# Float64 weights to float32 on the chip: another sequence of operations per piece

## The chip, the cores and the metric

The kernel runs on one core of one Trainium2 chip. The metric is the device time of one execution in microseconds (us), of which less is better. A core has a matrix engine (TensorE, PE in the profile, with its weight loads as PEld), a vector engine (VectorE, DVE), a scalar engine (ScalarE, ACT), a general engine (GpSimd, POOL) and a queue that here only issues DMAs (SyncE, SP). Each engine works through its own instructions in order; they wait for one another by semaphores.

## The reference

Attention with queries pooled in pairs, then two feed-forward blocks:

```python
q_pool = q.reshape(B, H, S // 2, 2, D).mean(axis=3)
attn = softmax(q_pool @ k.T / sqrt(D))            # 16 heads, 576 queries, 1152 keys, D = 64
x = (attn @ v) as [1152 tokens, 512]
h = x @ w_in                                      # MoE 1: 512 -> 2048 -> 512
x = where(h > 0, h, exp(min(h, 0)) - 1) @ w_out
xn = x / sqrt(mean(x * x) + 1e-6) * rms_g         # MoE 2: 512 -> 1536 -> 512
y = (silu(xn @ w_gate) * (xn @ w_val)) @ w_out2
```

The activations are float32. The five weight matrices arrive as float64 and are brought to float32 on the chip.

## The kernel before

Every float32 matrix is split into two float32r parts (a rounded one and the rest), and each product is three matmuls (lines 168 to 170). A weight is worked on in 68 pieces of [128, 512] words: 16 of `w_in`, 16 of `w_out`, 12 each of the gate, value and output weights of MoE 2. `Stream` (line 72) turns a piece into parts operation by operation. For one piece it records, with a `yield` after each: one ACT operation on the upper words (`Square`, line 111), a DVE shift (line 113), then the last three steps of the piece before (permission to take the buffers of its parts, an ACT copy to the rounded part `wh` at line 142, a POOL subtraction to the rest `wl` at line 62), and then five more DVE operations (lines 118, 121, 124, 126, 130). That makes 10 steps, six of them DVE operations on 128x512. The raw words are in `wr` (two buffers, loaded by SP, line 89), the results in `wt` (two buffers), helpers in `we` (two) and `wx` (one).

What the rest of the program does decides where these steps fall: `ws.step(i, k)` (line 149) records up to k of them between other work, and nothing if the next step would take a buffer of parts that is not allowed yet. With piece i in use, the stream may go as far as piece i + 8 (`WB`).

- Attention (lines 475 to 501): 72 tiles, 9 to a pair of heads. A tile has 6 score matmuls (L280), a scaled copy with its minimum on DVE (L284), the exponential on ACT (L289), 9 transposes (L298), copies on ACT (L306) and subtractions on DVE (L68), and 8 matmuls with v (L324). POOL splits q, k and v for the pair to come. In the last 33 tiles one step of the stream falls to each.
- MoE 1 hidden, first half and second half (line 593): 8 blocks by 3 chunks of 384 tokens each; 12 matmuls a chunk, then `elu` (line 181): two ACT operations, one DVE operation (L188), an ACT copy and a subtraction on POOL (in the second half on DVE for one chunk in three). Four steps of the stream per chunk.
- MoE 1 out, first half and second half (line 603): 24 products of 12 matmuls in each half, four steps of the stream per product, fewer at the end of the second half, where sums of squares (`Norm`, L562 to L569) are formed between the products.
- MoE 2 (line 646): pairs of products with `swiglu`, then the output products. Seven steps per pair.

A product's results go to one of 8 PSUM banks. PE may run ahead of the others by those banks; the out products need all hidden blocks.

## Time and profile before

| | |
|---|---|
| three timed runs | 724.67, 725.07, 725.17 us, median 725.07 |
| span of the profiled execution | 722.7 us |
| PE busy | 689.2 us (95%), 4243 matmuls |
| DVE busy | 614.9 us (85%), 965 instructions |
| ACT busy | 415.6 us (58%), 855 instructions |
| POOL busy | 390.7 us (54%), 326 instructions |

The span runs from the first to the last instruction of one more execution, taken with the profiler; about 2.4 us of a timed run lie outside of it. A busy engine is one whose instruction has started and not ended, waiting inside the instruction included. Matmuls overlap, so their count in a stretch says more than their busy time. The profile's stages, by the lines that run in them: attention 0 to 256 us, MoE 1 hidden first half 256 to 322, its out products to 368, hidden second half to 437, out products and norm to 506, MoE 2 to the end.

### The profile page before, as it was taken

Reading aid. Unit: us, or ns where it says so; the run is one execution under the profiler, and the core shown is the slowest. Engines: PE = TensorE matmul, PEld = TensorE weight load, DVE = VectorE, ACT = ScalarE, POOL = GpSimd, SP = SyncE. Lnnn points to the kernel's source line nnn. Section 1 sums busy time; section 2 is a strip of 40 time slices with the busy share of each in tenths; the row PEclk is TensorE's granted clock in tenths of the full one; section 3 lists DMA queues with packets and bytes.
Section 4 is the critical chain, followed back from the end, with each engine's and each line's share of the span. In section 5 each row is a group of like instructions: output and inputs, shape, how many; then the busy total and the mean of one; then the engine's idle time right before and its main releaser. Section 6 shows DMA issues by size and latency. Waiting matters only on the chain.

```text
span 722.7 us, 11547 instructions
## 1 busy us (share of the span) xinstructions
PE 689.2 (95%) x4243; PEld 673.3 (93%) x4243; DVE 614.9 (85%) x965; ACT 415.6 (58%) x855; POOL 390.7 (54%) x326
## 2 busy tenths in 40 slices
PE   7999999999999999969999968979999999999997
PEld 6999999989899999859999968979999999999997
DVE  7988989898999869999999999955999999999700
ACT  5888988889798865663356663424444443432300
POOL 4988889788896226754335453523445544443300
PEclk9999999999999999989999998989999999999999
DMA  5333322533331001223322212200222222222300
GB/s 196 116 96 135 98 84 83 172 131 107 105 98 48 1 30 60 87 70 105 117 92 85 87 59 88 88 30 1 87 88 89 88 88 88 88 88 88 124 34 33
DMA packets 21607, 62.34 MB, mean 86 GB/s; under 512 B 2736, under 2 KB 4784, under 8 KB 21552
## 3 DMA queue, kind: packets, MB, share of 16 engines
q1 hardware_dynamic: 21552, 61.62, 25.9%
q8 instruction: 33, 0.54, 0.3%
q14 instruction: 22, 0.18, 0.1%
HBM read 59.25 MB, written 2.36 MB: 85 GB/s over the span
## 4 chain that ended last, share of the span: by engine, by line
PE 74%; DVE 19%; ACT 3%; issue 3%; DMA 1%; SPq 0%; POOL 0%; DVEq 0%; ACTq 0%; POOLq 0%
PE b L169 15%; PE b L168 15%; PE b L170 15%; PE s L280 10%; PE o L324 9%; PE t L298 8%; DVE wt L121 3%; DVE wt L118 3%; DVE p L284 2%; DVE ptl L68 2%; DVE e L188 2%; DVE wx L124 2%; DVE wx L126 1%; DVE wt L130 1%; DVE wt L113 1%
## 5 line engine op out<-in xcount | busy, mean ns | idle before, releaser
L62 POOL TENSOR_TENSOR wl<-wt,wh 128x512 fp32r<-128x512 f32 x68 | 106.1, 1561 | 111.6 <-ACT wh L142 60.2
L168 PE MATMUL b<-xh,wh 128*128 128x384 f32 x468 | 157.7, 337 | 2.1 <-DVE e L188 1.5
L170 PE MATMUL b<-xh,wl 128*128 128x384 f32 x468 | 157.3, 336 | 0.0
L169 PE MATMUL b<-xl,wh 128*128 128x384 f32 x468 | 157.1, 336 | 0.0
L284 DVE TENSOR_SCALAR_CACHE_REDUCE p<-s 128x1152 f32<-128x1152 f32 x72 | 97.2, 1352 | 17.5 <-PE s L280 17.4
L68 DVE TENSOR_TENSOR ptl<-t,pth 128x384 fp32r<-128x384 f32 x216 | 106.5, 547 | 2.7 <-ACT pth L306 2.0
L280 PE MATMUL s<-kd,qt 128*128 128x384 f32 x480 | 98.6, 343 | 5.4 <-DVE p L284 4.8
L306 ACT CAST pth<-t 128x384 fp32r<-128x384 f32 x216 | 89.2, 488 | 24.1 <-PE t L298 23.5
L121 DVE SCALAR_TENSOR_TENSOR wt<-we,wt 128x512 f32<-128x512 f32 x68 | 95.5, 1404 | 4.5 <-ACT sqm L562 0.5
L289 ACT ACTIVATE p<-p,st 128x1152 f32<-128x1152 f32 x72 | 91.4, 1269 | 5.8 <-DVE p L284 5.5
L168 PEld LDWEIGHTS b<-xh,wh 128*128 128x128 f32 x468 | 88.0, 188 | 3.5 <-DVE e L188 2.5
L280 PEld LDWEIGHTS s<-kd,qt 128*128 128x128 f32 x480 | 81.5, 188 | 9.3 <-DVE p L284 6.5
L170 PEld LDWEIGHTS b<-xh,wl 128*128 128x128 f32 x468 | 88.0, 188 | 0.3 <-POOL wl L62 0.3
L169 PEld LDWEIGHTS b<-xl,wh 128*128 128x128 f32 x468 | 88.0, 188 | 0.0
L298 PE MATMUL t<-ident,p 128*128 128x128 f32 x648 | 85.3, 275 | 0.1
L324 PE MATMUL o<-pth,vd 128*128 128x256 f32 (+1 forms) x288 | 84.4, 315 | 0.0
L298 PEld LDWEIGHTS t<-ident,p 128*128 128x128 f32 x648 | 74.0, 141 | 6.3 <-DVE ptl L68 3.9
L324 PE MATMUL o<-ptl,vd 128*128 128x256 f32 (+1 forms) x288 | 78.5, 295 | 0.0
L168 PE MATMUL b<-gh,wh 128*128 128x384 f32 x180 | 64.3, 357 | 14.1 <-ACT gh L189 10.8
L142 ACT CAST wh<-wt 128x512 fp32r<-128x512 f32 x68 | 42.1, 619 | 59.5 <-DVE wt L130 58.4
L111 ACT ACTIVATE we<-wr 128x512 f32<-128x512 f32 x68 | 45.8, 674 | 47.2 <-DMA wr<-in_w_dram 16.1
L62 POOL TENSOR_TENSOR gl<-e,gh 128x384 fp32r<-128x384 f32 x37 | 46.8, 1265 | 41.4 <-ACT gh L189 39.7
(114 smaller groups left out, 1414.5 us busy)
## 6 DMA issues: line engine op xcount, KB each, us to landing
wr<-in_w_dram SPq DMA_DIRECT2D x32, 512.0 KB, 3.2
rawk<-in_k_dram SPq DMA_DIRECT2D x32, 288.0 KB, 2.9
rawq<-in_q_dram SPq DMA_DIRECT2D x15, 576.0 KB, 3.9
wr<-in_wg_dram SPq DMA_DIRECT2D x12, 512.0 KB, 3.2
wr<-in_wv_dram SPq DMA_DIRECT2D x12, 512.0 KB, 3.2
wr<-in_wo_dram SPq DMA_DIRECT2D x12, 512.0 KB, 3.3
rawv<-in_v_dram SPq DMA_DIRECT2D x16, 288.0 KB, 2.8
out_dram<-o SPq DMA_DIRECT2D x12, 192.0 KB, 1.9
```

Of the source, the lines that this page charges most:

```text
L62: G.tensor_tensor(out=o, in0=i, in1=f(h), op=ALU.subtract)
L68: V.tensor_tensor(out=o, in0=i, in1=f(h), op=ALU.subtract)
L121: V.scalar_tensor_tensor(out=f(t), in0=e, scalar=TINY64 * TINY64, in1=f(t), op0=ALU.is_ge, op1=ALU.mult)
L168: PE.matmul(out, lhsT=wh[:, k, :], rhs=ah, start=first and k == 0, stop=False)
L169: PE.matmul(out, lhsT=wh[:, k, :], rhs=al, start=False, stop=False)
L170: PE.matmul(out, lhsT=wl[:, k, :], rhs=ah, start=False, stop=last and k == 3)
L280: PE.matmul(s[:, m, 0:384], lhsT=a, rhs=b[:, 384 * m:384 * m + 384], start=n == 0, stop=n == len(parts) - 1)
L284: V.tensor_scalar(out=pt, in0=s[:, :, 0:384], scalar1=-0.0625, scalar2=None, op0=ALU.mult, op1=ALU.min, accum_out=st[p][:, 0, TILES[i][4], :])
L289: T.activation(out=pt, in_=pt, func=AF.Exp, scale=-1.0, bias=st[p][:, 0, TILES[i][4], :], accum_out=st[p][:, 1, TILES[i][4], :])
L298: PE.transpose(ps[:, k, :], src[:, 128 * b:128 * b + 128], ident)
L306: T.copy(oh, re(ps))
L324: PE.matmul(self.o[:, 0:self.N], lhsT=v[:, b, :], rhs=(pth, ptl)[u][:, g["buf"], b, g["c0"]:320], start=self.n == 0, stop=self.n == 17)
```

## The change

A piece is brought to float32 by another sequence. On ACT, `Abs` of an eighth of the upper words goes straight to `wt`. On DVE: the lower words, scaled and added to a constant, to `we`; `wt` limited from both sides; `wt` shifted left by three bits; the sign merged in from the upper words; and an integer add of `wt` and `we`. That is five DVE operations instead of six: three with one tensor input, one with two, and the add. `wx` is gone. The steps of a piece are 9 instead of 10. The rest of the kernel stands as it was (its comments are gone, which shifts lines by one or two).

```diff
-                    e = wp.tile([128, 512], F32, tag="we", name="we", bufs=2)
+                    e = wp.tile([128, 512], U32, tag="we", name="we", bufs=2)
                     t = wp.tile([128, 512], U32, tag="wt", name="wt", bufs=2)
-                    x = wp.tile([128, 512], U32, tag="wx", name="wx", bufs=1)
-                    T.activation(out=e, in_=f(hi), func=AF.Square)
+                    T.activation(out=f(t), in_=f(hi), func=AF.Abs, scale=0.125)
                     yield
-                    V.tensor_scalar(out=t, in0=hi, scalar1=3, scalar2=0x3FFFFFF8,
-                                    op0=ALU.logical_shift_left, op1=ALU.bitwise_and)
+                    V.tensor_scalar(out=f(e), in0=lo, scalar1=2.0 ** -27, scalar2=2.0 ** 25,
+                                    op0=ALU.mult, op1=ALU.add)
                     yield
                     if tail:
                         yield from tail
-                    V.scalar_tensor_tensor(out=t, in0=hi, scalar=0xC0000000, in1=t,
-                                           op0=ALU.bitwise_and, op1=ALU.bitwise_or)
+                    V.tensor_scalar(out=f(t), in0=f(t), scalar1=LEAST64, scalar2=MOST64, op0=ALU.max, op1=ALU.min)
                     yield
-                    V.scalar_tensor_tensor(out=f(t), in0=e, scalar=TINY64 * TINY64, in1=f(t),
-                                           op0=ALU.is_ge, op1=ALU.mult)
+                    V.tensor_scalar(out=t, in0=t, scalar1=3, scalar2=None, op0=ALU.logical_shift_left)
                     yield
-                    V.tensor_scalar(out=x, in0=t, scalar1=0xFF800000, scalar2=None, op0=ALU.bitwise_and)
-                    yield
-                    V.scalar_tensor_tensor(out=f(x), in0=lo, scalar=2.0 ** -52, in1=f(x), op0=ALU.mult, op1=ALU.mult)
+                    V.scalar_tensor_tensor(out=t, in0=hi, scalar=0x80000000, in1=t,
+                                           op0=ALU.bitwise_and, op1=ALU.bitwise_xor)
                     self.load(i + 3)
                     yield
+                    V.tensor_tensor(out=t, in0=t, in1=e, op=ALU.add)
                     w = f(t)
-                    V.tensor_tensor(out=w, in0=w, in1=f(x), op=ALU.add)
```

Since `ws.step` counts steps, the instructions also move. In attention two of the stream's loads come ahead of a load of v on SP's queue that they stood behind. Three other places show what moves. `e` is elu's tile, `b` a PSUM bank, `wt`, `we`, `wx` and `wr` the stream's.

DVE in MoE 1's first hidden half, from its first chunk; before:

```order
L188 SCALAR_TENSOR_TENSOR e_3553<-e_3553,b_3540 128x384
L118 SCALAR_TENSOR_TENSOR wt_3510<-wr_3053,wt_3510 128x512
L121 SCALAR_TENSOR_TENSOR wt_3510<-we_3509,wt_3510 128x512
L124 TENSOR_SCALAR wx_3511<-wt_3510 128x512
L126 SCALAR_TENSOR_TENSOR wx_3511<-wr_3053,wx_3511 128x512
L188 SCALAR_TENSOR_TENSOR e_3578<-e_3578,b_3565 128x384
L130 TENSOR_TENSOR wt_3510<-wt_3510,wx_3511 128x512
L113 TENSOR_SCALAR wt_3590<-wr_3501 128x512
L188 SCALAR_TENSOR_TENSOR e_3606<-e_3606,b_3593 128x384
```

and now:

```order
L187 SCALAR_TENSOR_TENSOR e_3544<-e_3544,b_3531 128x384
L120 TENSOR_SCALAR wt_3496<-wt_3496 128x512
L122 TENSOR_SCALAR wt_3496<-wt_3496 128x512
L124 SCALAR_TENSOR_TENSOR wt_3496<-wr_2921,wt_3496 128x512
L128 ISA wt_3496<-wt_3496,we_3495 128x1024
L187 SCALAR_TENSOR_TENSOR e_3569<-e_3569,b_3556 128x384
L115 TENSOR_SCALAR we_3579<-wr_3310 128x512
L187 SCALAR_TENSOR_TENSOR e_3596<-e_3596,b_3583 128x384
```

A piece's conversion ends one elu earlier, and the integer add stands there as an instruction of its own kind over 1024 elements a partition, the half-words of 512 words. From the first elu to the last of this half there are 51 operations of the stream on DVE before and 45 now.

DVE in MoE 1's second hidden half, three chunks in its middle; before:

```order
L113 TENSOR_SCALAR wt_4791<-wr_4714 128x512
L188 SCALAR_TENSOR_TENSOR e_4809<-e_4809,b_4796 128x384
L118 SCALAR_TENSOR_TENSOR wt_4791<-wr_4714,wt_4791 128x512
L121 SCALAR_TENSOR_TENSOR wt_4791<-we_4790,wt_4791 128x512
L68 TENSOR_TENSOR gl_3539<-e_4809,gh_3538 128x384
L124 TENSOR_SCALAR wx_4792<-wt_4791 128x512
L126 SCALAR_TENSOR_TENSOR wx_4792<-wr_4714,wx_4792 128x512
L188 SCALAR_TENSOR_TENSOR e_4834<-e_4834,b_4821 128x384
L130 TENSOR_TENSOR wt_4791<-wt_4791,wx_4792 128x512
L113 TENSOR_SCALAR wt_4846<-wr_4769 128x512
L188 SCALAR_TENSOR_TENSOR e_4862<-e_4862,b_4849 128x384
```

and now:

```order
L115 TENSOR_SCALAR we_4715<-wr_4640 128x512
L69 TENSOR_TENSOR gl_3530<-e_4705,gh_3529 128x384
L187 SCALAR_TENSOR_TENSOR e_4732<-e_4732,b_4719 128x384
L187 SCALAR_TENSOR_TENSOR e_4751<-e_4751,b_4738 128x384
L120 TENSOR_SCALAR wt_4716<-wt_4716 128x512
L122 TENSOR_SCALAR wt_4716<-wt_4716 128x512
L124 SCALAR_TENSOR_TENSOR wt_4716<-wr_4640,wt_4716 128x512
L128 ISA wt_4716<-wt_4716,we_4715 128x1024
L187 SCALAR_TENSOR_TENSOR e_4776<-e_4776,b_4763 128x384
```

With 9 steps to a piece the stream has come to the end of its buffers by here: after five operations in two chunks comes a chunk with none. In the whole half there are 56 operations of the stream before and 40 now.

ACT in the first hidden half, at the start of a piece, with the engines and queues that an instruction waits for; before:

```order
L189 CAST gh_3538<-e_3553 128x384 [waits DVE_49]
L111 ACTIVATE we_3589<-wr_3501 128x512 [waits DMAHW0_49]
L184 ACTIVATE e_3606<-b_3593 128x384 [waits PE_49,Pool_49]
L185 ACTIVATE e_3606<-e_3606 128x384 [waits Activation_49]
L189 CAST gh_3538<-e_3578 128x384 [waits DVE_49]
```

and now:

```order
L188 CAST gh_3529<-e_3544 128x384 [waits DVE_49]
L113 ACTIVATE wt_3580<-wr_3310 128x512 [waits DMAHW0_49,Pool_49]
L183 ACTIVATE e_3596<-b_3583 128x384 [waits PE_49]
L184 ACTIVATE e_3596<-e_3596 128x384 [waits Activation_49]
L188 CAST gh_3529<-e_3569 128x384 [waits DVE_49]
```

The ACT operation on the upper words stands at the same place, but it writes `wt` now and waits for POOL's subtraction on the piece two before, which reads the same buffer.

## Rows read from the trace of the kernel before

**Rows 1.** Windows: stretch, length, busy us (instructions) per engine, TensorE clock, DMA share, GB/s.

```profile
262.00:322.00 60.00, 52.80 (x298) 51.20 (x296) 56.31 (x71) 40.72 (x85) 39.12 (x30) 0.99 0.22 71
300.00:330.00 30.00, 22.41 (x107) 20.74 (x106) 29.52 (x37) 16.85 (x35) 19.85 (x15) 0.89 0.22 71
330.00:360.00 30.00, 30.00 (x174) 30.00 (x173) 28.48 (x40) 11.65 (x22) 8.75 (x7) 1.00 0.33 109
368.00:437.00 69.00, 59.81 (x333) 57.74 (x332) 65.27 (x92) 45.41 (x94) 34.63 (x26) 0.98 0.26 85
410.00:440.00 30.00, 20.81 (x101) 18.81 (x100) 28.15 (x41) 17.87 (x38) 14.99 (x12) 0.90 0.21 71
460.00:480.00 20.00, 15.39 (x79) 14.98 (x78) 13.76 (x20) 6.45 (x13) 8.09 (x7) 0.83 0.16 54
506.00:690.00 184.00, 184.00 (x1060) 184.00 (x1059) 169.53 (x232) 70.25 (x137) 80.46 (x55) 1.00 0.27 90
```

**Rows 2.** Waits of PE: who for whom, us in total, times, longest.

```profile
PE b L168 <- ACT gh L189: 10.8, 2, 5.6
PE b L569 <- DVE sq L564: 5.4, 2, 4.6
PE b L168 <- DVE e L188: 4.8, 5, 1.7
```

**Rows 3.** Chain of work that ended last, shares by line, 396 to 437 us.

```profile
by line: issue 19.4%; DVE wt L118 17.3%; DVE wt L121 16.7%; DVE e L188 13.7%; DVE wx L124 8.1%; DVE wt L130 6.9%; DVE wx L126 5.4%; DVE gl L68 5.2%; DVE wt L113 3.5%; PE b L169 1.7%; ACT wh L142 1.5%; ACT gh L189 1.3%; POOL gl L62 1.2%; DVE
```

**Rows 4.** The clock while PE starts again: windows of 1 us.

```profile
321.00:322.00 1.00, 0.28 (x1) 0.28 (x1) 0.97 (x3) 0.84 (x2) 0.77 (x2) 0.63 0.00 0
327.00:328.00 1.00, 1.00 (x5) 1.00 (x4) 1.00 (x1) 0.22 (x1) 1.00 (x2) 0.50 0.07 16
```

**Rows 5.** Durations by line: ns min/median/max, first and last start us, shape.

```profile
L113 DVE TENSOR_SCALAR wt<-wr x68: 409/419/1266, 141.4 to 677.8; 128x512 uint32<-128x512 uint32 x68
L118 DVE SCALAR_TENSOR_TENSOR wt<-wr,wt x68: 671/693/1545, 144.5 to 678.3; 128x512 uint32<-128x512 uint32 x68
L121 DVE SCALAR_TENSOR_TENSOR wt<-we,wt x68: 678/1591/1675, 148.4 to 679.1; 128x512 f32<-128x512 f32 x68
L124 DVE TENSOR_SCALAR wx<-wt x68: 411/428/1405, 151.8 to 680.7; 128x512 uint32<-128x512 uint32 x68
L126 DVE SCALAR_TENSOR_TENSOR wx<-wr,wx x68: 629/693/1649, 155.5 to 681.1; 128x512 f32<-128x512 uint32 x68
L130 DVE TENSOR_TENSOR wt<-wt,wx x68: 630/691/1550, 158.8 to 681.9; 128x512 f32<-128x512 f32 x68
```

**Rows 6.** Timeline: start us, us, instruction; DVE and POOL around 283 us.

```profile
282.73 1.01 POOL L62 TENSOR_TENSOR gl<-e,gh 128x384 fp32r<-128x384 f32 x1 [2.37 <-ACT gh L189]
282.82 1.46 DVE L118 SCALAR_TENSOR_TENSOR wt<-wr,wt 128x512 uint32<-128x512 uint32 x1
283.70 1.74 POOL L62 TENSOR_TENSOR wl<-wt,wh 128x512 fp32r<-128x512 f32 x1
284.32 1.67 DVE L121 SCALAR_TENSOR_TENSOR wt<-we,wt 128x512 f32<-128x512 f32 x1
```

**Rows 7.** Groups of DVE: elu's operation (busy us, mean ns | idle before, releaser).

```profile
L188 DVE SCALAR_TENSOR_TENSOR e<-e,b 128x384 f32<-128x384 f32 x45 | 24.5, 545 | 0.8 <-ACT e L185 0.8
```

**Rows 8.** Durations by line, as in rows 5: POOL's subtractions, and ACT's first operation.

```profile
L62 POOL TENSOR_TENSOR wl<-wt,wh x68: 1263/1704/1850, 178.8 to 683.4; 128x512 fp32r<-128x512 f32 x68
L62 POOL TENSOR_TENSOR gl<-e,gh x37: 1001/1316/1464, 271.2 to 440.6; 128x384 fp32r<-128x384 f32 x37
L111 ACT ACTIVATE we<-wr x68: 641/674/694, 138.4 to 676.4; 128x512 f32<-128x512 f32 x68
```

**Rows 9.** Chain, start us and us: one tile of each pair of heads.

```profile
100.15 2.11 PE s L280 x12
130.02 2.11 PE s L280 x12
161.61 2.36 PE s L280 x12
```

More of the change, by code (lines that the diff above doesn't have):

```diff
@@ L23 @@
 DM = 512
-TINY64 = float.fromhex("0x1.2p-15")
+LEAST64, MOST64 = 2.0 ** -18, float.fromhex("0x1.dffffep+13")
 TILES = [(1, 128, 0, 64, 1), (1, 256, 0, 192, 3), (None, 0, None, 0, 8), (1, 384, 1, 64, 5), (1, 512, 1, 192, 7),
```

## The prediction

> **What bounds the kernel now.** I read the windows first, by matmul counts, since matmuls overlap and busy shares hide half speed. In MoE 2 PE is never idle: 1060 matmuls in 184 us, and 174 in the 30 us after 330 us [rows 1]. That is the full rate; what DVE saves under it brings nothing. Against 174 per 30 us (0.172 us each), three stretches fall short: 107 from 300 to 330 us (67 missing, 11.6 us), 101 from 410 to 440 us (73, 12.6 us), 79 instead of 116 from 460 to 480 us (37, 6.4 us) [rows 1]. Together 30.6 us; this is the ground on which a lighter stream can win.
>
> The waits of PE say for whom: twice, up to 5.6 us, for a `gh` copy, which itself follows DVE's elu operation; five times for that operation directly; and 4.6 us of 5.4 us in one piece for DVE's sum of squares [rows 2]. The chain in the second stretch lies on DVE, most of it on the stream's own lines (L118, L121, L124, L130) [rows 3]. So in both hidden halves PE runs ahead on its banks, then waits for an elu that stands in DVE's queue behind the stream.
>
> Part of the loss is the clock. After 5.2 us without work PE comes back at half speed: 0.63 in the first microsecond, still 0.50 at 327 us [rows 4]; the mean is 0.89, 0.90 and 0.83 over the three stretches [rows 1]. About 5.4 us at half speed in the first stretch cost 2.7 us.
>
> Why DVE is slow there: the stream's operations have two kinds of length. One tensor input takes 419 or 428 ns, two take 691 to 693 ns in the median and 678 at least for L121, whose median is 1591 [rows 5]. The rest is waiting for POOL: L118 starts 0.09 us after a POOL subtraction and ends 0.54 us after its end; L121 begins during the next subtraction and ends 0.55 us after that one [rows 6].
>
> **The change part by part.**
>
> *Removed and added on DVE.* A piece costs 419 + 693 + 691 + 428 + 693 + 691 = 3615 ns before without waits (for L121 I take L130's 691) [rows 5]. After it: three one-input operations at 420, one merge at 693 as L118, and the add. The add exists nowhere in the trace. It covers the same 512 words from two tensors as L130, so 691 if it goes word by word; it stands in the program with 1024 elements, and a DVE operation on two tensors goes from 545 ns at 384 elements to 691 at 512 [rows 5, 7], 1.14 ns an element, so 1275 ns if it goes half-word by half-word. I take 691, the row of the instruction that it replaces, with 1275 as the other end. A piece is then 3 x 420 + 693 + 691 = 2644 ns, 0.97 us less; 0.529 us an operation against 0.602.
>
> The Trainium skill ("VectorE: DVE Perf Modes", the perf-mode tier table) gives two-input operations on 16-bit data two elements a cycle where 32-bit data get one; by it the add would be an operation of 512 cycles, thus L130's length. No run here shows it yet.
>
> *First hidden half, 262 to 322 us.* DVE is busy 56.3 of 60 us with 71 instructions [rows 1]: 22 elus at 0.545 [rows 7] = 12.0 us, and 49 of the stream in the other 44.3 us, 0.904 each, 0.30 of it waiting. The order has 51 such operations from the first elu to the last before and 45 after. If each keeps its wait, 51 x 0.904 = 46.1 becomes 45 x 0.829 = 37.3, 8.8 us less. If instead the waits keep their sum (51 x 0.302 = 15.4 us), because POOL's work causes them and is not reduced (one subtraction more falls into the half, 9 pieces instead of 8.4, some 0.6 us), it is 45 x 0.529 + 16.0 = 39.8, 6.3 us less. I take 6.3: the waits ended with POOL's instructions in each of the cases in rows 6. PE would then restart at 316.5 rather than 322.8 us. It has used up its work at 316.5, so its idle time is small, and the clock should not fall: 2.7 us more. Sum 9.0 of at most 11.6 us.
>
> On the choice between the two sums the Trainium skill ("SBUF — State Buffer", section "SBUF: two separate sides") has a rule: DVE and GpSimd share a pair of ports, which a DVE operation in a two-port mode or with two SBUF inputs takes for itself as a whole, as GpSimd's does. It speaks against the change, since the three one-input operations also take the pair and POOL's share is untouched. Rows 6 agree with it (0.54 and 0.55 us after POOL's end). By it the saving is the 6.3 us, by each operation keeping its wait it would be 8.8, and the whole time 2.5 us lower.
>
> *Second hidden half, 368 to 437 us.* Here the count falls more, since the stream has reached the end of its buffers: 56 operations become 40. DVE is busy 65.3 us with 92 instructions [rows 1], 23 elus (12.5 us) and 7 subtractions like elu's in length (3.8 us) among them; 62 of the stream in 49.0 us, 0.79 each. Sixteen fewer are 12.6 us, and 40 x 0.073 are 2.9: 15.5 us, more than the 12.6 us that are lost. I take 12.0 of them.
>
> *Sums of squares, 460 to 480 us.* The sum of squares stands in DVE's queue behind what is left of the stream. Some 4 pieces fall between, as before, each 0.97 us shorter, and the backlog from the hidden half is gone. Of 6.4 us I take 5.8.
>
> *Attention, last 33 tiles.* A pair of heads takes 31.59 us with the stream in it (130.02 to 161.61) and 29.87 without [rows 9], 6.2 us over 3.6 pairs for 20 DVE operations, 0.31 each. There are 20 again, but five more of them have one input: 5 x 0.27 = 1.4 us of DVE, of which I count 0.5. The two loads moved ahead of v's loads on SP can cost POOL some tenths; not counted.
>
> *ACT.* `Abs` for `Square` is one operation of the same size [rows 8]; I give it the same 674 ns. Its new wait, for POOL's subtraction two pieces before, holds up what stands behind it on ACT: the next chunk's two elu operations and `gh` copies, for which DVE and then PE wait. I cost it at nothing: between that subtraction and `Abs` stand four DVE operations of the piece before (2.2 us) against a subtraction of 1.7 us [rows 8]. If that cover is gone it is a rival, below.
>
> Sum: 9.0 + 12.0 + 5.8 + 0.5 = 27.3 us. The span of 722.7 becomes 695.4; a timed run is about 2.4 above the span, so **698 us** (median 725.07 less 27.3 is 697.8).
>
> **The rivals.**
>
> 1. *The gain is half* (add at 1275 ns, or waits that grow as much): 0.58 us a piece comes back. With 9 pieces in the first half 6.3 - 5.2 = 1.1 us, and the clock falls as before; second half 15.5 - 8 x 0.58 = 10.9; sums 5.8 - 2.3 = 3.5; attention -0.4. Sum 15.1, 710 us. For it: the 1024 elements in the order. Against: the bytes are the same.
>
> 2. *One-input operations do not take 420 ns* in the added forms (float32 arithmetic, or integer shifts in place): at 690 each, 0.81 us a piece comes back, and the change then hardly does what it looks like: -1.0, 9.0, 2.6 and -0.7, sum 9.9, 715 us. Against: L113 reads with gaps and L124 does not, and both take 420 [rows 5].
>
> 3. *Slower: `Abs` waits for POOL.* If ACT is held at each piece for a whole subtraction, 1.74 us [rows 6], in 9 + 8 + 4 pieces of MoE 1, 36.5 us come onto elu's path against 27.3 saved: 734 us. It decides from 1.3 us a piece. For it: in rows 6 the subtraction runs from 283.70, and ACT reaches its operations well ahead of DVE. Against: ACT is busy 40.7 of 60 us there [rows 1], and the banks let PE run on.
>
> 4. *All of it comes back*: the 30.6 us and 2 us in attention, 692 us. For it: the 8.8 us sum above and 15.5 against 12.6.
>
> **How the numbers follow.** Forecast 0.60, with 691 to 705 around it (the first half between 6.3 and 11.6, one stretch missed by half); rival 4 has 0.10, rival 1 0.16, rival 2 0.07, rival 3 0.05, no effect 0.02. The range leaves out rival 3, most of rival 2 and the far ends: 689 to 713. A measurement of this kernel can tell about 0.2% (1.5 us) from no change. Faster than that: 0.60 + 0.10 + 0.16 + 0.07 = 0.93; within it 0.02; slower 0.05.
>
> **What would show it right or wrong.** In the profile after: the one-input lines at 420 ns at least, merge and add at 690; 45 and 40 stream operations in the hidden halves; near 170 matmuls in each 30 us of MoE 1 hidden, and no clock under 0.95 in a stretch after 300 us; PE's waits for `gh` and for the sum of squares under 1 us; MoE 2 as long as before, 184 us. An add with a least time over 1.2 us means rival 1, one-input lines at 690 rival 2, long waits of ACT's first line for POOL rival 3. Wrong altogether would be a forecast in which PE still waits 5 us for `gh`: then POOL, not DVE's operations, sets elu's pace.

## The result, and the profile after

The changed kernel takes **702.31 us** in the median (701.97 to 702.84), the kernel before beside it 724.93 (724.67 to 725.17). The ratio is 0.9677, with an interval from 0.9659 to 0.9695: 3.2% faster, 22.6 us. The forecast was 698, the gain 27.3. The span fell from 722.7 to 700.6 us.

The page of the changed kernel, busy time and share of the span of each engine, and the shares of the engines in the chain that ended last:

```profile
PE 682.1 (97%) x4243; PEld 669.4 (96%) x4243; DVE 546.2 (78%) x897; ACT 416.0 (59%) x855; POOL 374.9 (54%) x326
PE 81%; DVE 12%; ACT 3%; POOL 1%; DMA 1%; issue 1%; SPq 0%; DVEq 0%; ACTq 0%; POOLq 0%
```

DVE's busy time fell by 69 us, the run by 22: some 41 us of what DVE saves lie in MoE 2 (177.6 to 136.6 us of DVE in a stage that takes 227.6 us in both kernels), under a PE that was never late. The windows of the changed kernel (stretch in us, length, busy us and instructions of PE, PEld, DVE, ACT, POOL, TensorE clock, DMA share, GB/s) answer to [rows 1]:

```profile
262.00:322.00 60.00, 53.73 (x303) 52.48 (x302) 53.61 (x65) 43.46 (x89) 37.76 (x31) 0.98 0.21 71
300.00:330.00 30.00, 23.73 (x119) 22.48 (x118) 29.03 (x37) 19.05 (x39) 19.47 (x17) 0.89 0.25 83
330.00:360.00 30.00, 30.00 (x174) 30.00 (x174) 29.00 (x41) 13.08 (x24) 13.52 (x9) 1.00 0.44 150
410.00:440.00 30.00, 30.00 (x173) 29.83 (x172) 28.75 (x43) 17.43 (x35) 14.00 (x10) 1.00 0.30 102
460.00:480.00 20.00, 19.24 (x118) 18.84 (x117) 10.01 (x19) 7.71 (x16) 5.37 (x6) 1.00 0.00 1
506.00:690.00 184.00, 184.00 (x1058) 184.00 (x1057) 107.09 (x170) 61.72 (x121) 58.62 (x47) 1.00 0.24 82
```

The second and the third stretch with losses are repaired: 173 matmuls instead of 101 from 410 to 440 us, 118 instead of 79 from 460 to 480, the clock at 1.00 in both. (The stages behind the first half begin 2 to 22 us earlier now, so the same window no longer holds the same work; the table by stages below agrees.) The first is not: 119 instead of 107 from 300 to 330 us, where full rate is 174, and the clock is 0.89 there as before. PE's waits say the same. Who waits for whom, us in total, times, longest, in the changed kernel (compare [rows 2]):

```profile
PE b L167 <- ACT gh L188: 4.6, 1, 4.6
PE b L168 <- POOL gl L63: 1.1, 1, 1.1
PE b L568 <- DVE sq L563: 0.8, 1, 0.8
PE b L167 <- DVE e L187: 0.6, 1, 0.6
```

One wait of 4.6 us for a `gh` copy is left, and it is that of the first half. The sum of squares is down from 5.4 to 0.8 us.

PE's instructions stand in the same order in both kernels, so the start of the same matmul can be compared. This table divides the profiled executions into stages by such starts: first score matmul, first matmul of an early hidden block, the first matmul of an out product that reads the first half's `gh` (the tenth of that product), the ninth matmul of the second half, the first of its out products, the first of MoE 2, and the last matmul's end. Each row is one trace. The experiments are in it too; they are told below.

| us | attention | hidden 1 | out 1 | hidden 2 | out 2 and norm | MoE 2 |
|---|---|---|---|---|---|---|
| before | 245.4 | 56.9 | 60.1 | 51.8 | 70.6 | 227.6 |
| after | 246.1 | 55.3 | 59.4 | 48.5 | 53.4 | 227.6 |
| e1_wt3 | 246.5 | 55.3 | 59.6 | 48.5 | 53.5 | 227.6 |
| e2_ten_steps | 243.4 | 55.1 | 53.1 | 48.5 | 53.7 | 227.6 |
| e3_before_nine | 252.2 | 61.0 | 62.4 | 56.0 | 65.7 | 229.7 |
| e4_later | 245.9 | 56.0 | 51.3 | 48.5 | 59.3 | 227.6 |
| e5_wl_dve | 247.5 | 55.1 | 58.3 | 48.5 | 53.4 | 227.7 |
| e6_attn | 249.4 | 55.3 | 60.0 | 48.5 | 53.4 | 227.6 |
| e7_gl_dve | 246.6 | 55.1 | 58.5 | 48.5 | 53.4 | 227.6 |
| e8_eleven | 242.8 | 56.8 | 51.2 | 48.5 | 55.7 | 227.6 |
| e9_two_inputs | 247.9 | 56.9 | 60.2 | 48.5 | 55.8 | 227.6 |
| e10_four_ops | 245.6 | 55.1 | 54.0 | 48.6 | 53.4 | 227.6 |
| e11_before_eleven | 246.1 | 62.7 | 55.6 | 48.5 | 69.5 | 227.6 |
| e12_three | 246.3 | 55.9 | 51.4 | 48.5 | 62.1 | 227.7 |

From before to after: attention -0.7, first half with its out products +2.3 (56.9 + 60.1 to 55.3 + 59.4), second half with out products and norm +20.4, MoE 2 nothing: 22.0 us, the difference of the spans within 0.1. A hidden half that runs late shows it in the column behind it, since PE runs ahead on its banks and waits at the start of the out products.

**The prices were as assumed.** Durations by line in the changed kernel: ns least/median/greatest, first and last start us, shape.

```profile
L113 ACT ACTIVATE wt<-wr x68: 648/677/705, 139.0 to 638.6; 128x512 f32<-128x512 f32 x68
L115 DVE TENSOR_SCALAR we<-wr x68: 365/418/1522, 142.0 to 636.6; 128x512 f32<-128x512 uint32 x68
L120 DVE TENSOR_SCALAR wt<-wt x68: 410/421/1530, 145.2 to 639.3; 128x512 f32<-128x512 f32 x68
L122 DVE TENSOR_SCALAR wt<-wt x68: 415/428/1406, 149.0 to 639.8; 128x512 uint32<-128x512 uint32 x68
L124 DVE SCALAR_TENSOR_TENSOR wt<-wr,wt x68: 673/1371/1670, 152.0 to 640.2; 128x512 uint32<-128x512 uint32 x68
L128 DVE CUSTOM_DVE_ANT_0 wt<-wt,we x68: 675/693/1670, 156.0 to 641.0; 128x1024 uint16<-128x1024 uint16 x68
```

The add takes 693 ns in the median for its 1024 half-words, 675 at least, as the 32-bit add that it replaces (691, [rows 5]). By the Trainium skill ("VectorE: DVE Perf Modes", the perf-mode tier table) a two-input operation makes two elements a cycle on 16-bit data and one on float32, so that, as an estimate from it, 1024 half-words cost what 512 words do. The trace agrees with that, 693 against 691 ns in the median, though the add stands in it as a custom instruction. The three one-input operations take 418, 421 and 428. With the merge at 693, whose median of 1371 is half waiting, a piece costs DVE 2.65 us of its own, against 3.615.

**Where the first half's gain went.** DVE's operations between the start of the first elu operation on that half's own banks and that of the last (20 chunks), by line: busy us, mean ns | idle before them. First the kernel before, 268.11 to 324.74 us:

```profile
L121 DVE SCALAR_TENSOR_TENSOR wt<-we,wt 128x512 f32<-128x512 f32 x8 | 13.3, 1666 | 0.3
L188 DVE SCALAR_TENSOR_TENSOR e<-e,b 128x384 f32<-128x384 f32 x20 | 10.9, 546 | 0.8 <-ACT e L185 0.8
L118 DVE SCALAR_TENSOR_TENSOR wt<-wr,wt 128x512 uint32<-128x512 uint32 x8 | 10.1, 1263 | 0.0
L126 DVE SCALAR_TENSOR_TENSOR wx<-wr,wx 128x512 f32<-128x512 uint32 x8 | 8.6, 1080 | 0.3
L124 DVE TENSOR_SCALAR wx<-wt 128x512 uint32<-128x512 uint32 x8 | 7.5, 943 | 0.1
L130 DVE TENSOR_TENSOR wt<-wt,wx 128x512 f32<-128x512 f32 x8 | 5.5, 687 | 0.1
L113 DVE TENSOR_SCALAR wt<-wr 128x512 uint32<-128x512 uint32 x8 | 3.4, 419 | 0.0
```

and the changed kernel, 268.38 to 323.50 us:

```profile
L124 DVE SCALAR_TENSOR_TENSOR wt<-wr,wt 128x512 uint32<-128x512 uint32 x9 | 12.3, 1371 | 0.2
L122 DVE TENSOR_SCALAR wt<-wt 128x512 uint32<-128x512 uint32 x9 | 12.3, 1368 | 0.2
L187 DVE SCALAR_TENSOR_TENSOR e<-e,b 128x384 f32<-128x384 f32 x21 | 11.5, 545 | 1.8 <-ACT e L184 1.8
L128 DVE CUSTOM_DVE_ANT_0 wt<-wt,we 128x1024 uint16<-128x1024 uint16 x9 | 9.0, 996 | 0.2
L120 DVE TENSOR_SCALAR wt<-wt 128x512 f32<-128x512 f32 x9 | 8.5, 944 | 0.0
L115 DVE TENSOR_SCALAR we<-wr 128x512 f32<-128x512 uint32 x9 | 3.8, 417 | 0.0
```

Eight pieces before, nine after, in the same 20 chunks. The sums of the stream are 48.4 and 45.9 us, of which the operations' own lengths are 8 x 3.615 = 28.9 and 9 x 2.65 = 23.9. The rest is waiting: 19.5 before, 22.0 after, in both kernels **2.44 us a piece**. The shift L122, 0.43 us long by itself, takes 1.37 there; the other 0.94 us are waiting. The stretch itself shrank by only 1.5 us, from 56.6 to 55.1, since DVE also stands idle 1.0 us longer, for elu's exponential on ACT.

### The profile page after: what moved, and what is told of

The parts are those of the page before. It is cut to its first block, busy times and chain, and to the rows that moved or that the text cites. A ratio compares the mean times of both kernels' runs of the same rounds, so it can differ in the third digit from the quotient of the medians.

```text
span 700.6 us, 11340 instructions
## 1 busy us (share of the span) xinstructions
PE 682.1 (97%) x4243; PEld 669.4 (96%) x4243; DVE 546.2 (78%) x897; ACT 416.0 (59%) x855; POOL 374.9 (54%) x326
## 4 chain that ended last, share of the span: by engine, by line
PE 81%; DVE 12%; ACT 3%; POOL 1%; DMA 1%; issue 1%; SPq 0%; DVEq 0%; ACTq 0%; POOLq 0%
PE b L168 17%; PE b L167 17%; PE b L169 17%; PE s L279 10%; PE o L323 9%; PE t L297 8%; DVE p L283 3%; DVE ptl L69 2%; DVE wt L124 2%; DVE wt L122 1%; DVE wt L120 1%; DVE e L187 1%; DMA rawk<-in_k_dram 1%; POOL wl L63 1%; DVE wt L128 1%
## 5 line engine op out<-in xcount | busy, mean ns | idle before, releaser
L63 POOL TENSOR_TENSOR wl<-wt,wh 128x512 fp32r<-128x512 f32 x68 | 99.8, 1467 | 72.8 <-ACT wh L141 53.8
L113 ACT ACTIVATE wt<-wr 128x512 f32<-128x512 f32 x68 | 46.0, 676 | 66.6 <-POOL wl L63 50.9
L124 DVE SCALAR_TENSOR_TENSOR wt<-wr,wt 128x512 uint32<-128x512 uint32 x68 | 80.5, 1184 | 1.8
L63 POOL TENSOR_TENSOR gl<-e,gh 128x384 fp32r<-128x384 f32 x37 | 44.9, 1215 | 45.8 <-ACT gh L188 45.8
L128 DVE CUSTOM_DVE_ANT_0 wt<-wt,we 128x1024 uint16<-128x1024 uint16 x68 | 65.8, 968 | 1.9
L167 PE MATMUL b<-gh,wh 128*128 128x384 f32 x180 | 62.0, 344 | 5.2 <-ACT gh L188 4.6
```

Of the source, the lines that this page charges most:

```text
L63: G.tensor_tensor(out=o, in0=i, in1=f(h), op=ALU.subtract)
L124: V.scalar_tensor_tensor(out=t, in0=hi, scalar=0x80000000, in1=t, op0=ALU.bitwise_and, op1=ALU.bitwise_xor)
L167: PE.matmul(out, lhsT=wh[:, k, :], rhs=ah, start=first and k == 0, stop=False)
```

## The experiments

Twelve kernels ran, each timed beside the kernel before in the same job (its medians there: 724.9 to 725.4 us). Times below are medians with their ratio to it. Three questions: is it a wait of ACT, the length or the number of DVE's operations, or POOL's share?

**e1_wt3: a third buffer for `wt`,** so that `Abs` need not wait for POOL's subtraction two pieces before.

```diff
-t = wp.tile([128, 512], U32, tag="wt", name="wt", bufs=2)
+t = wp.tile([128, 512], U32, tag="wt", name="wt", bufs=3)
```

> The changed kernel with three buffers of wt in place of two, so that ACT's first operation on a piece no longer waits for POOL's subtraction on the piece two before. Theory P (port): in the first hidden half DVE's operations take turns with POOL's subtractions, and that alone sets the pace; ACT's wait is covered. Then PE comes back at 319 to 320 us as in the changed kernel and the time is 701.5 to 702.8 us (changed kernel: 702.3). Theory A (Abs): the wait, 5.9 us in seven pieces between 262 and 322 us, delays elu's two ACT operations behind it and has eaten the gain of the first half. Then PE comes back by 315 us, its clock does not fall, and the time is 695 to 698 us.

702.83 us, ratio 0.9696 (0.9678 to 0.9715): no change. The wait had been there. ACT's waits from 262 to 322 us, in the changed kernel:

```profile
ACT gh L188 <- DVE e L187: 6.3, 8, 1.3
ACT wt L113 <- POOL wl L63: 5.9, 7, 1.2
```

and with the third buffer:

```profile
ACT gh L188 <- DVE e L187: 11.6, 8, 2.2
```

The 5.9 us for POOL's `wl` are gone, and ACT waits 5.3 us more for DVE's elu instead. Theory P has the time, and rival 3 the mechanism but not the price: ACT had this time to spare.

**e2_ten_steps: one empty step in each piece** (a tenth, after the shift). Nothing else differs from the changed kernel.

```diff
                     V.tensor_scalar(out=t, in0=t, scalar1=3, scalar2=None, op0=ALU.logical_shift_left)
                     yield
+                    yield
```

> The changed kernel with an empty tenth step in each piece, so that the stream goes on at the pace of before: 43, 50 and 47 of its operations on DVE in first hidden half, out products and second hidden half, against 45, 55 and 40. It tells the price of the operations from their number. Theory M (price): cheaper operations are enough in the second half, 47 of them at 0.78 us and 16 us of other DVE work are 53 us beside 49 us of PE and its lead of some 8 us; time 701 to 704 us. Theory C (count): the second half gained because the stream had reached the end of its buffers there; with 47 in place of 40 about half of the 13 us is lost again, time 707 to 710 us.

**694.22 us**, ratio 0.9578 (0.9557 to 0.9598): 8.1 us better than the changed kernel, which neither theory had expected. Its window over the stretch that had stayed slow, and PE's waits in MoE 1:

```profile
300.00:330.00 30.00, 28.06 (x156) 26.86 (x155) 29.41 (x39) 17.53 (x36) 17.56 (x14) 1.00 0.33 106
...
PE b L169 <- POOL gl L63: 1.3, 3, 0.8
PE b L569 <- DVE sq L564: 0.8, 1, 0.8
PE b L168 <- ACT gh L189: 0.6, 1, 0.6
```

The clock stays at 1.00, the wait for `gh` is 0.6 us. In the stage table 6.3 us come from "out 1" (where the first half's wait lies) and 2.8 from attention, with nothing lost later. In 20 chunks there are 8 pieces again, as before.

**e3_before_nine: the kernel before in nine steps** (lines 124 and 126 in one step), with all its dear operations.

```diff
                     V.tensor_scalar(out=x, in0=t, scalar1=0xFF800000, scalar2=None, op0=ALU.bitwise_and)
-                    yield
                     V.scalar_tensor_tensor(out=f(x), in0=lo, scalar=2.0 ** -52, in1=f(x), op0=ALU.mult, op1=ALU.mult)
```

> The kernel before with the operations of lines 124 and 126 in one step, so that a piece has 9 steps but all six dear operations: 54, 66 and 48 of them in first hidden half, out products and second hidden half, against 51, 60 and 56. Theory M (price): without cheaper operations the pace gains little; the first half ends 3 x 0.90 = 2.7 us later, the second gains 8 x 0.78 = 6.3 us at most, less what 66 x 0.78 = 51 us in the out products of 49 us leave over; 721 to 726 us. Theory C (count): the end of the buffers brings the second half's 13 us as it did in the changed kernel, time 712 to 716 us.

739.86 us, ratio 1.0197 (1.0169 to 1.0224): 14.7 us slower. Both theories miss: the higher of their ranges ends at 726. With e2 this makes a square of the change's two parts:

| us | dear operations | cheap operations |
|---|---|---|
| ten steps | 725.2 (before) | 694.2 (e2) |
| nine steps | 739.9 (e3) | 702.3 (after) |

The cheaper operations bring 31.0 us at ten steps and 37.6 at nine. The missing step costs 14.7 us with dear operations and 8.1 with cheap ones. The change did both at once.

**e4_later: fewer steps in the first half, more behind it.** Three steps a chunk in the first half instead of four, five per out product there instead of four.

```diff
-        ws.step(wi, 2)
+        ws.step(wi, 1 if wi < 8 else 2)
...
-                    ws.step(wi + q, 4)
+                    ws.step(wi + q, 4 if hf else 5)
```

> The changed kernel with three steps per chunk in place of four in the first hidden half and five per product in place of four in its out products: 35, 65 and 40 operations of the stream against 45, 55 and 40. Theory P: ten operations fewer are 10 x 0.97 = 9.7 us less for DVE before PE comes back; the idle 6.3 us between 300 and 322 us go and the clock does not fall (2.7 us): 693 to 696 us. Theory A: two of nine waits for POOL go with the pieces, some 1.5 us, and PE still waits: 699 to 702 us.

700.57 us, ratio 0.9664 (0.9646 to 0.9682). The time is in theory A's range, but not by its reason. The first half is repaired, as theory P had it (out 1 from 59.4 to 51.3), but 5.9 us come back in "out 2" (53.4 to 59.3). I read this as the out products' 65 operations running over into the second half; e12 was to test that.

**e5_wl_dve and e7_gl_dve: less work on POOL.** e5 has the stream's subtraction to `wl` on DVE for pieces 3 to 12, e7 elu's subtraction to `gl` for one chunk in three of the first half.

```diff
-            lo_pool(l2, w, h2)
+            (lo_dve if NE <= i < 13 else lo_pool)(l2, w, h2)
```

```diff
-                elu(ps, gh[:, i, cs(c)], gl[:, i, cs(c)], lo_dve if c == 1 and hf else lo_pool)
+                elu(ps, gh[:, i, cs(c)], gl[:, i, cs(c)], lo_dve if c == 1 else lo_pool)
```

> The changed kernel, with the stream's subtraction to wl moved from POOL to DVE for pieces 3 to 12, those of MoE 1's first hidden half and the start of its out products. In the first half POOL then has only the subtractions of elu. Theory W (DVE waits for whatever POOL subtracts, wl as much as gl): a piece costs DVE 4.9 us there now, 2.3 of it waiting; one POOL operation of 1.5 us in three goes, so the waits fall by about 1.0 and DVE's own work rises by 0.7: first half 1 to 3 us shorter, 699 to 701 us. Theory G (only the subtractions of elu matter, since they come at every chunk): the waits stay, DVE has 0.7 us more a piece, 9 pieces: 6 us longer, 706 to 710 us, and PE waits over 6 us for gh at the start of the out products.

> The changed kernel, with elu's subtraction to gl on DVE instead of POOL for one chunk in three of the first hidden half too, as it stands in the second half. The number of the stream's operations at each place is unchanged. Theory W (DVE's waits follow POOL's work): POOL loses 8 operations of 1.17 us, 9.3 us, DVE gains 8 of 0.55 us, 4.4 us; the pace of elu in the first half goes from 2.73 us a chunk to about 2.5, PE waits under 2 us for gh there: 696 to 699 us. Theory C (DVE's count alone sets the pace): DVE has more to do, 2.9 us a chunk, PE waits 7 us or more for gh: 703 to 707 us.

701.94 us, ratio 0.9667 (0.9642 to 0.9692), and 702.19 us, ratio 0.9677 (0.9650 to 0.9705): neither changes anything. But the waits did fall. The lines of e5 for the merge, the shift and the subtraction, from the first elu to the last:

```profile
L69 DVE TENSOR_TENSOR wl<-wt,wh 128x512 fp32r<-128x512 f32 x9 | 8.9, 987 | 3.8 <-ACT wh L141 3.8
L122 DVE TENSOR_SCALAR wt<-wt 128x512 uint32<-128x512 uint32 x9 | 8.6, 960 | 0.2
L124 DVE SCALAR_TENSOR_TENSOR wt<-wr,wt 128x512 uint32<-128x512 uint32 x9 | 8.3, 922 | 0.2
```

The shift is down from 1368 to 960 ns, the merge from 1371 to 922. In e5 a piece's five operations wait 1.1 us instead of 2.44, in e7 1.6 (worked out as above). So the waits do come from POOL's subtractions, as theory W said. The Trainium skill ("SBUF — State Buffer", section "SBUF: two separate sides") has a rule for it: a DVE operation in a two-port mode or with two SBUF inputs and a GpSimd operation that reads SBUF take a shared pair of ports in turn, each for its whole length. The trace agrees as far as it goes: with less work on POOL the waits fell to 1.1 and 1.6 us a piece.

The time does not follow. In e7 the pace of elu (the mean time from one elu operation to the next) stays, 2.78 us a chunk against 2.76: DVE has more subtractions itself, 5.5 us, and stands 3.5 us idle before them, because their input comes from ACT, which had waited for DVE. In e5 the pace does get better, 2.58, so that the 20 chunks take 51.6 us instead of 55.1. But the first of them starts 3.1 us later (271.44 us instead of 268.38): attention is 1.4 us longer in that trace, and a first subtraction now stands before that elu on DVE, after 1.7 of the 3.8 us of idle time for ACT's `wh`. The last elu comes only 0.5 us sooner, and PE still waits 4.4 us for `gh`. Neither theory had counted this hand-over.

**e6_attn: the steps in attention at every second one of the last 66 tiles** instead of each of the last 33.

```diff
-        ws.step(0, step >= ns - 33)
+        ws.step(0, step >= ns - 66 and (ns - step) % 2)
```

> The changed kernel, with the stream's 33 steps in attention spread over its last 66 tiles, one at every second tile, instead of one at each of the last 33. The same operations before MoE 1. Theory N (each operation of the stream delays attention by a fixed piece, whatever lies around it): 702 us, within 1. Theory D (attention has some slack per tile, and it is the density that costs): of the 2 to 3 us that the stream costs attention most comes back, 699.5 to 701 us, with the shift of PE's instructions at 250 us showing it.

704.89 us, ratio 0.9711 (0.9686 to 0.9736): 2.6 us slower than the changed kernel. The stage table has it all in attention (246.1 to 249.4, in a trace of the slowest of its four runs, 706.14 us). Both theories miss: spread thin, the stream costs more there. Why is not settled.

**e8_eleven: two empty steps in each piece.**

```diff
                     yield
+                    yield
+                    yield
                     V.scalar_tensor_tensor(out=t, in0=hi, scalar=0x80000000, in1=t,
```

> The changed kernel with two empty steps in each piece, 11 instead of 9 (the run with one empty step took 694.2 us). Theory M (fewer pieces per chunk is what helps, and ten steps already take PE's waits in the first half away): nothing more to win in the first half, attention has fewer operations of the stream again, 692 to 695 us, all of it by 260 us. Theory T (ten steps fit because two pieces fall on five chunks evenly, nine and eleven leave chunks with four waiting operations): PE waits 3 us or more for gh in the first half again, 697 to 702 us.

695.59 us, ratio 0.9584 (0.9561 to 0.9607), just above theory M's range (692 to 695) and below theory T's. PE does not wait for `gh`, so the first half needs no even pattern of two pieces in five chunks: elu's pace is 2.39 us a chunk against 2.42 in e2. It is not better than ten steps, because the third piece now comes late for the early blocks (hidden 1 56.8 instead of 55.1) and the norm waits a little (55.7 instead of 53.7).

**e9_two_inputs: the shift on two tensors** (an or with zeros), so that one operation is 0.27 us longer, with number and order unchanged. The lines that make and clear the tile of zeros are left out here. It tests a simpler theory that e1 to e8 had suggested: in the first half the stream's operations took 1.01 to 1.02 us in the mean in before, after, e2, e3 and e4, so perhaps only their number counts.

```diff
-                    V.tensor_scalar(out=t, in0=t, scalar1=3, scalar2=None, op0=ALU.logical_shift_left)
+                    V.scalar_tensor_tensor(out=t, in0=t, scalar=3, in1=zero,
+                                           op0=ALU.logical_shift_left, op1=ALU.bitwise_or)
```

> The changed kernel with the left shift as an operation on two tensors (the second is all zeros and is merged in by an or): about 0.69 us by itself instead of 0.42, 0.27 us more a piece; the number and the order of operations stay. Theory C (in the first hidden half an operation of the stream takes 1.01 to 1.02 us with its wait, whatever its own length, as in five kernels so far, so that only their number counts): elu's pace there stays at 2.76 us a chunk, the stream's operations stay at 1.02 us in the mean; what the longer shift costs it costs later, 702 to 704 us. Theory L (own length plus a wait that stays the same, as in the prediction): 9 pieces by 0.27 us in the first half and as much in the second, pace 2.87 us, 706 to 709 us.

708.88 us, ratio 0.9772 (0.9755 to 0.9789). Theory C falls. The shift in the first half:

```profile
L123 DVE SCALAR_TENSOR_TENSOR wt<-wt,zero 128x512 uint32<-128x512 uint32 x9 | 14.7, 1636 | 0.2
```

1636 instead of 1368 ns: the longer length stands in full on top of the same wait, and elu's pace goes from 2.76 to 2.88 us a chunk, theory L's number. The four other lines did not move by more than 3 ns.

**e10_four_ops: without the limits on the magnitude** (left out; its step stays, empty), so four operations in nine steps.

```diff
-                    V.tensor_scalar(out=f(t), in0=f(t), scalar1=LEAST64, scalar2=MOST64, op0=ALU.max, op1=ALU.min)
```

> The changed kernel without the operation that limits the magnitudes from both sides (left out, with its step kept empty): four DVE operations in nine steps, 1.78 a chunk instead of 2.22 (with the one empty step of the ten-step kernel: 2.0). Theory C (number alone): 36 operations instead of 45 from the first elu to the last of the first half, 9 by 1.02 us; elu's pace falls from 2.76 us a chunk to the 2.4 at which ACT holds it in the runs with spare time, PE does not wait for gh there, 693 to 696 us. Theory L (own length, the waits as they were): 0.42 us by 9 pieces, 3.8 us, pace 2.57, PE still waits 1 to 3 us for gh, 697 to 700 us.

696.07 us, ratio 0.9595 (0.9581 to 0.9609). The time lies between the ranges (693 to 696, and 697 to 700), the pace at 2.47 us a chunk between theory C's 2.4 and theory L's 2.57, and PE's wait for `gh`, 0.2 us, speaks for C. Per piece the wait is 2.23 us instead of 2.44: it fell, but by less than the 0.49 us that an operation's even share would be. This run alone does not decide between the two; e9 and e11 do.

**e11_before_eleven: the kernel before with an empty step,** which gives the dear operations at nearly the changed kernel's number (45 from the first elu to the last in both).

```diff
                     V.tensor_scalar(out=x, in0=t, scalar1=0xFF800000, scalar2=None, op0=ALU.bitwise_and)
                     yield
+                    yield
```

> The kernel before with one empty step in each piece, 11 steps with its six dear operations: 2.18 operations a chunk, as the changed kernel has (2.22). Theory C (number alone): the first hidden half from the first elu to the last takes what the changed kernel takes, 54 to 56 us, against 56.6 before; with the second half (51 operations instead of 56) and less in attention 713 to 718 us. Theory L (length): 44 operations that are 0.073 us longer each than in the changed kernel, 57 to 59 us there, 719 us or more.

720.33 us, ratio 0.9932 (0.9912 to 0.9952). From the first elu to the last it takes 58.0 us, the changed kernel 55.1: at the same number of operations the cheaper ones are worth 2.9 us, theory L again.

**e12_three: as e4, but with four steps per out product.**

```diff
-        ws.step(wi, 2)
+        ws.step(wi, 1 if wi < 8 else 2)
```

> The changed kernel with three steps of the stream per chunk in the first hidden half, as in the run that gave 700.6 us, but with four per product in the out products as before, not five. The stretch from the first elu to the last of the first half then holds 7 pieces (35 operations), not 9. Theory P (a piece costs DVE 2.64 us of its own and 2.45 us of waiting, wherever POOL subtracts for elu; the run with five steps lost its gain because 65 operations did not fit into the 50 us of the out products and ran over into the second half): the first half without a wait for gh, elu's first operation of the second half right after its product, in the second half 48 operations instead of 40, 9.7 pieces by 5.1 us, 2.5 us a chunk, PE waits 0 to 2 us: 694 to 697 us. Rival Q (the second half ends late whatever happens, once PE comes to it earlier): PE waits 3 us or more for gh at its end and loses the clock, 699 to 702 us.

703.21 us, ratio 0.9686 (0.9668 to 0.9704), above both ranges. PE waits 4.2 us for `gh`, which is rival Q's sign, though not by its reason. The overflow of e4 was real. The first elu operation of the second half, first in e4, then in e12 (start us, us, instruction [idle before it]):

```profile
366.02 0.56 DVE L187 SCALAR_TENSOR_TENSOR e<-e,b 128x384 f32<-128x384 f32 x1 [1.16 <-ACT e L184]
...
361.94 0.55 DVE L187 SCALAR_TENSOR_TENSOR e<-e,b 128x384 f32<-128x384 f32 x1 [2.47 <-ACT e L184]
```

But the second half then has 50 operations of the stream where the changed kernel has 40, at a pace of 2.75 us a chunk, as in the changed kernel's first half, and the loss stands there. The window of e12 at the end of its second half:

```profile
410.00:440.00 30.00, 24.52 (x123) 23.95 (x122) 28.59 (x42) 16.41 (x33) 13.28 (x11) 0.89 0.30 105
```

123 matmuls where the changed kernel has 173, and the clock at 0.89. So at nine steps the second half is whole **because** the stream had run to the end of its buffers by then, which the overfed first half paid for. At ten steps that is not needed: e2's second half has 47 operations at a pace of 2.47 us and loses nothing (out 2 53.7). This table has the waits of the runs side by side (first half; stretch from the first elu's start to the last's, in us; a piece counts by its operations, so it can be a fraction). In e1 and e6 the stretch is as in the changed kernel, in e12 as in e4:

| | steps, operations per piece | us for 20 chunks | pieces | own length, sum | with waits | wait per piece |
|---|---|---|---|---|---|---|
| before | 10, 6 | 56.6 | 8 | 28.9 | 48.4 | 2.44 |
| after | 9, 5 | 55.1 | 9 | 23.9 | 45.9 | 2.44 |
| e2_ten_steps | 10, 5 | 48.5 | 8 | 21.2 | 40.5 | 2.41 |
| e3_before_nine | 9, 6 | 63.6 | 9 | 32.5 | 54.6 | 2.45 |
| e4_later | 9, 5 (three a chunk) | 48.9 | 7 | 18.6 | 35.6 | 2.43 |
| e5_wl_dve | 9, 5 (`wl` on DVE) | 51.6 | 9 | 23.9 | 33.8 | 1.10 |
| e7_gl_dve | 9, 5 (more `gl` on DVE) | 55.6 | 9 | 23.9 | 38.0 | 1.57 |
| e8_eleven | 11, 5 | 47.7 | 7.4 | 19.6 | 38.7 | 2.58 |
| e9_two_inputs | 9, 5 | 57.5 | 9 | 26.2 | 48.2 | 2.44 |
| e10_four_ops | 9, 4 | 49.3 | 9 | 20.1 | 40.2 | 2.23 |
| e11_before_eleven | 11, 6 | 58.0 | 7.5 | 27.1 | 49.2 | 2.95 |

## Why the prediction was right, and where it was not

**Sign and size of the whole were right** (22.6 us of 27.3; inside the range and inside the forecast's own 691 to 705). The sum was not right term by term: the first half gave 6.7 us less than forecast, the second half and the sums of squares 2.6 us more, attention 1.2 us less. That the total stayed in the range was in part luck.

**The step that failed is the first hidden half:** 9.0 us forecast, 2.3 measured. Its working was 51 operations at 0.904 us against 45 with the waits' sum kept, 6.3 us, and 2.7 us of clock. What the runs show instead:

- The count. Of the 51 operations three stand between the early blocks' elus, where nothing is late; in the dense stretch there are 48 against 45. Three operations at 0.60 us of their own: 1.8 us.
- The waits. I kept their sum (15.4 us, and 0.6 for a little more of POOL's work). They are a sum per **piece**, and the whole ninth piece brings its 2.44 us: 19.5 to 22.0 in the dense stretch. The table shows 2.41 to 2.45 in six kernels whose own lengths per piece differ from 2.65 to 3.615 us (2.58, 2.23 and 2.95 in e8, e10 and e11). With 2.5 instead of 0.6: 1.9 us.
- DVE's idle time for ACT grew by 1.0 us. These three make 4.7 of the 4.8 us by which 6.3 became 1.5.
- The clock. I wrote that PE's idle time would be small and the clock would not fall. PE still waits 4.6 us for `gh`, and the clock is 0.89 from 300 to 330 us as before: the 2.7 us did not come. Some 0.8 us were gained outside of the dense stretch.

Behind all of it is one thing that I saw in the order and priced only as "one subtraction more": nine steps to a piece instead of ten put a ninth piece, 5.1 us of DVE's time with its waits, into a half that was already late. I took the count of operations for the load; the load is pieces times (own length plus wait). e2, which gives the tenth step back and changes nothing else, has 8 pieces, 48.5 us and no stall: with the operations' price alone the first half brings 8.8 us of the 9.0 forecast (hidden 1 and out 1: 117.0 to 108.2).

What exactly holds elu at 2.76 us a chunk at nine steps is **not settled**. The chain of waits in the changed kernel (start us, us, what) leaves DVE once in nine chunks, for 6.4 us:

```profile
284.45 1.40 DVE wt L128
285.86 0.02 issue
285.88 0.62 ACT wh L141
286.50 0.40 ACT e L183
...
287.35 0.51 ACT gh L188
...
287.93 1.01 POOL gl L63
288.94 1.43 POOL wl L63
...
290.39 0.68 ACT wt L113
...
292.25 0.54 DVE e L187
```

The add hands a piece to ACT, ACT's copies and POOL's two subtractions follow, `Abs` waits for `wl`, and elu's two ACT operations stand behind `Abs`. That is rival 3's path. With the wait taken away (e1) the pace stays 2.76, with elu's subtractions partly off POOL (e7) it is 2.78 and with the same rotation in the second half (e12) 2.75: when one engine is relieved, the next stands at the same point. But it is no fixed pace of nine steps: with `wl` off POOL (e5) it is 2.58, with four operations (e10) 2.47, with a longer shift (e9) 2.88. "Wrong altogether" in the prediction named this case, PE still waiting 5 us for `gh`, and laid it to POOL; POOL alone it is not, by e5 and e7.

**Second half and sums of squares:** 12.0 + 5.8 = 17.8 us forecast, 20.4 measured (51.8 + 70.6 to 48.5 + 53.4). The mechanism was right, 56 operations become 40 and the backlog before the sums of squares goes; the terms were slightly small. What I had not seen is that the 40 depend on the first half: with 50 at nine steps (e12) 8.7 us come back, while 47 at ten steps (e2) cost 0.3. At nine steps the two halves are not two gains but one stream: relieved in the first half, it is late in the second.

**Attention:** 0.5 forecast, -0.7 measured, from one trace each; the changed kernel and four others with the same attention (e1, e4, e7, e12) lie between 245.9 and 246.6, a spread as large as this loss. The square shows two large parts that cancel: at nine steps the cheap operations bring 6.1 us (252.2 to 246.1), and with dear operations the missing step costs 6.8 (245.4 to 252.2). I took "20 again" for no change, but the 33 steps hold 3.7 pieces instead of 3.3.

**ACT** at nothing was right in its sum: `Abs` takes 677 ns, and its wait, though there, costs nothing by e1. **Rivals 1 and 2** fall by the rows of L128 and of the one-input lines. **Rival 4** falls by the 4.6 us wait; e2 comes to 2.2 us from its 692.

Of the signs that I had named, the one-input lines, merge and add, the 45 and 40 operations, the sum of squares under 1 us and an unchanged MoE 2 came true (227.6 us in both); the 170 matmuls and the clock from 300 to 330 us did not, nor did a wait for `gh` under 1 us (4.6).

**The version to keep is e2_ten_steps**: 694.22 us against 702.31 and 724.93, the changed kernel with one empty step.

## What to carry to other kernels

When work is fed in by steps, a change that removes a step also raises the feed; count whole units of work in each stage, with the waits that a unit brings, not instructions. Test price and pace apart (an empty step is enough), since one can hide part of the other (here 8.1 us of 31.0). And a stage that became fast because a queue in front of it was full can owe its gain to the stage that filled it.

## What was unexpected of the hardware

- In the first half DVE's waits beside POOL were 2.41 to 2.45 us per piece in six kernels, whether the piece's own operations took 2.65 or 3.6 us, and an operation of 0.43 us waited as long as one of 0.69 (the shift took 1368 ns, on two inputs 1636). Three other kernels with the same work on POOL per chunk had 2.23, 2.58 and 2.95 (e10, e8, e11). A shorter operation saves its own length there and nothing of the wait.
- Taking a subtraction from POOL cut these waits by half (2.44 to 1.1 us a piece in e5) and made the 20 chunks 3.6 us shorter, without any gain in the run's time.
- The same number of steps of the stream in attention cost 3.3 us more when spread over twice the tiles (e6, one trace; 2.6 us in the medians).
